# Two layers of local attention and a bilinear unit on one core: the down weights' loads move from SyncE's DMA queue to GpSimd's

## The chip, the cores and the metric

The kernel runs on one core of one Trainium2 chip. The core has five engines with instruction queues of their own: TensorE (PE, matrix products; its weight loads are shown as PEld), VectorE (DVE), ScalarE (ACT), GpSimd (POOL) and SyncE (SP). DMAs are issued by an engine's queue and carried out by 16 DMA engines. The metric is the device time of one execution in microseconds (us), the median of several runs.

## The reference

The model has four half-layers on 2048 tokens of width D = 576, in bfloat16: attention, gated unit, attention, gated unit, each with a layer norm ahead and a residual behind. The attention looks at 8 positions, 2 apart, with 32 heads of 18 elements:

```python
def _A_ref(x, wqkv, wo):
    qkv = (x @ wqkv).reshape(B, S, 3, H, Dh)          # H = 32, Dh = 18
    idx = pos[:, None] - arange(8)[None, :] * 2        # position and seven before it
    logits = einsum("bhsd,bhswd->bhsw", q, k[idx]) * Dh ** -0.5   # masked where idx < 0
    o = einsum("bhsw,bhswd->bhsd", softmax(logits), v[idx])
    return o.reshape(B, S, D) @ wo

def _B_ref(x, w_gate, w_up, w_down):                   # F = 4608
    return ((x @ w_gate) * (x @ w_up)) @ w_down

x = x + _A_ref(layernorm(x), wqkv, wo)
x = x + _B_ref(layernorm(x), w_gate, w_up, w_down)
x = x + _A_ref(layernorm(x), wqkv, wo)
x = x + _B_ref(layernorm(x), w_gate, w_up, w_down)
```

All four use the same weights A and B.

## The kernel before

The 2048 tokens are 16 tiles of 128. They are worked on in 18 *sequences*; a sequence is one attention and the gated unit after it for one or two tiles. The first four have one tile each, the other 14 have two (256 tokens). All intermediate results stay on the chip. The gate and up weights (wg, wu, wgu_t) are loaded once, in six parts; the down weights (5.3 MB) do not fit beside them and are loaded anew in every sequence, 18 loads of 288 KB each (`load_wd`, L682), 324 in all, into six buffers wd0 to wd5 taken in turn.

*Gated unit* (`glu`, L632). A unit of work has 512 columns of PSUM: gate matmuls (L655, into pg), up matmuls (L655, into pu), the tails of the 576 rows (L666), then ACT copies the gate half (g_sb, L677) and DVE multiplies (h, L678). Units come in threes. After some units come the down matmuls of the same units (L699 with 512 columns, L700 with 64), and DVE adds the residual (L709, L714). This is a phase. A one-tile sequence has three phases of three units, a two-tile sequence two phases of nine units. A one-tile phase needs six loads, as many as there are buffers. A two-tile phase has nine loads, all entered into the plan ahead of the phase's first down step; the last three of them go over buffers that the first three have just filled, and wait for nothing but those landings. The down steps of the first three units and of the last three then read the same buffers.

*Attention* (`attention`, L378). Projections on PE (L407); on DVE, products of q with shifted k (L503) and their sums (L507 to L512); score sums over a head's elements on PE (L518); softmax on DVE and ACT (L540 to L551, result s); then the weights are brought to all rows of a head: in the first five sequences by PE (L557), in the other thirteen through DRAM (a_dram, L567, and four DMAs back into ab, L570). DVE multiplies with v and adds (L587, L602), PE multiplies with wo (L614), DVE adds the residual (L620). The layer norm ahead of each half is DVE statistics (L343), ACT (L349, L358), and a transpose on PE (L369, first five sequences) or by DMA (L362).

*Order.* Nothing is issued as it is written. Every step is entered with `op`: its engine, a cost in ns, the buffers that it reads and writes, and a priority. `Plan.run` (L69) then goes through the ready steps, takes the one that can start first by these costs, and emits it. So each engine's order of instructions, PE's too, is fixed when the kernel is built, from the planned costs; on the chip each engine takes its instructions in that order and waits by semaphores. A DMA is planned as an issue on SP, then bytes at 250 GB/s after whatever DMA was planned before, then 2000 ns (L114 to L116):

```python
if o.nbytes:
    dma = max(dma, o.end) + o.nbytes / 250.0
    o.ready = dma + 2000
```

Before the change SP issues every DMA: inputs, weights, the trips of the attention weights through DRAM, DMA transposes, the down weights and the output. A load of wd waits in SP's queue until PE has read the buffer's old content, and until the DMA eight issues earlier has landed. POOL has only fills and masks at the start.

The diff touches `Plan.run` and `load_wd` in `glu`; the kernel's main loop calls `attention` and `glu` for each sequence and then `Plan.run`.

Of the kernel before, what the change touches and what calls it, by code (L numbers as in the profile page):

```python
# [20 lines left out]
class Plan:  # L21
# [11 lines left out]
    def op(self, eng, cost, fn, r=(), w=(), prio=1, after=None, hold=None, free=None, margin=0, nbytes=0, use=None,  # L33
           pair=None, need=None):
        o = Op()
        o.eng, o.cost, o.fn, o.prio, o.hold, o.free = eng, cost, fn, prio, hold, free
        o.margin, o.idx, o.succ, o.order, o.nbytes = margin, len(self.ops), [], set(), nbytes
        o.lat, o.use, o.pair, o.need = self.LAT[eng], use, pair, need
        d = set()
        for k in r:  # L40
            d.update(self.wr.get(k, ()))
        for k in w:
            d.update(self.wr.get(k, ()))
            d.update(self.rd.get(k, ()))
        for k in r:
            self.rd.setdefault(k, []).append(o)
        for k in w:
            self.wr[k] = [o]
            self.rd[k] = []
        d.discard(o)  # L50
        o.deps = d
        if after is not None and after not in d:
            o.order.add(after)
        for p in d | o.order:
            p.succ.append(o)
        o.n = len(d | o.order)
        self.ops.append(o)
        return o
# [9 lines left out]

    def run(self, slots):  # L69
        clock = {e: 0.0 for e in self.LAT}  # L70
        dma = 0.0
        free = {k: [(0.0, i) for i in range(v)] for k, v in slots.items()}
        cand = [o for o in self.ops if o.n == 0]
        done = 0
        while cand:
            best = None
            for o in cand:
                t = 0.0
                for p in o.deps:
                    e = p.ready if p.eng != o.eng else p.end  # L80
                    if e > t:
                        t = e
                t += o.margin
                if o.hold is not None:
                    f = free[o.hold]
                    if not f:
                        continue
                    t = max(t, min(f)[0])
                if o.pair is not None:
                    if len(free["unit"]) < len(o.pair):  # L90
                        continue
                    t = max(t, min(free["unit"])[0])
                if o.need is not None:
                    t = max(t, o.need["at"])
                t = max(t, clock[o.eng])
                key = (t, o.prio, o.idx)
                if best is None or key < best[0]:
                    best = (key, o)
            assert best is not None, "the plan is stuck"
            (t, _, _), o = best  # L100
            cand.remove(o)
            if o.hold is not None:
                got = min(free[o.hold])
                free[o.hold].remove(got)
                o.use["slot"] = got[1]
            if o.pair is not None:
                for u in o.pair:
                    got = min(free["unit"])
                    free["unit"].remove(got)
                    u["at"], u["slot"] = got  # L110
            o.end = t + o.cost
            clock[o.eng] = o.end
            o.ready = o.end + o.lat
            if o.nbytes:  # L114
                dma = max(dma, o.end) + o.nbytes / 250.0
                o.ready = dma + 2000  # L116
            if o.free is not None:
                u = o.use
                u["last"] = max(u.get("last", 0.0), o.ready)
                u["left"] = u.get("left", 1) - 1  # L120
                if u["left"] == 0:
                    free[o.free].append((u["last"], u["slot"]))
            o.fn()
            done += 1
            for s in o.succ:
                s.n -= 1
                if s.n == 0:
                    cand.append(s)
        assert done == len(self.ops)
# [3 lines left out]
def kernel(  # L133
# [12 lines left out]
    nc = tc.nc  # L146
    _, S, D = A_x.shape
    F = B_w_gate.shape[1]
    P = 128
# [17 lines left out]
    NXS, NWD, NH, NXB, NB = 4, 6, 9, 3, 3  # L167
# [6 lines left out]
    wd_v = B_w_down.rearrange("(g t p) d -> g p t d", p=P, t=2)  # L174
# [5 lines left out]
    def sb(name, shape, dt=BF16):  # L180
        return consts.tile(shape, dt, name=name)
# [30 lines left out]
    wd = [sb(f"wd{i}", [P, 2, D]) for i in range(NWD)]  # L212
# [12 lines left out]
    op = pl.op  # L225
# [23 lines left out]
    def dma(dst, src):  # L249
        return lambda: nc.sync.dma_start(dst, src)  # L250
# [376 lines left out]
    wd_no = {"n": 0}  # L627
# [4 lines left out]
    def glu(j, t0, nst, last):  # L632
        n = nst * P
# [48 lines left out]
        def load_wd(g):  # L682
            b = wd_no["n"] % NWD
            wd_no["n"] += 1
            op("SP", 550, dma(wd[b][:], wd_v[g]), w=[f"wd{b}"], nbytes=P * 2 * D * 2, prio=5.5 + (g // 3 if j == 0 else 0))
            return b

        nph = 2 if nst == 2 else 3
# [32 lines left out]
        for ph in range(nph):  # L721
            hsl, wsl = {}, {}
            mine = range(ph * upp, (ph + 1) * upp)
            for u in range(ph * upp, (ph + 1) * upp, NB):
                us = (u, u + 1, u + 2)
                for m in us:
                    wsl[m] = [load_wd(m * fpu // 2 + g) for g in range(fpu // 2)]
                    units[m] = {}
                full(u, wg, "wg", pg, True, False, pair=tuple(units[m] for m in us))
                full(u, wu, "wu", pu, True, False)  # L730
                full(u + 1, wg, "wg", pg, True, False, need=units[u + 1])
                tails(us)
                hsl[u] = evac(u)
                full(u + 1, wu, "wu", pu, False, True)
                hsl[u + 1] = evac(u + 1)
                full(u + 2, wg, "wg", pg, False, True)
                full(u + 2, wu, "wu", pu, False, True)
                hsl[u + 2] = evac(u + 2)
            use = {"left": nst}
            for m in mine:  # L740
                down(m, hsl[m], wsl[m], ph, use)
            settle(ph, use)
# [52 lines left out]
```

## Time and profile before

| | us |
|---|---|
| median of 3 runs | 1096.94 (1095.88 to 1098.84) |
| the profiled execution | 1094.6 |
| its span, first to last instruction | 1092.5 |
| PE busy | 1057.1 |
| DVE busy | 761.4 |
| ACT busy | 364.1 |
| POOL busy | 5.9 (26 instructions) |
| wd: 324 loads, median from issue to landing | 3.4 |

The profile is one execution as the hardware recorded it. A row of a group names the line, the engine, the operation and its tiles, the count, then busy time and mean duration, then the engine's idle time ahead of these instructions and what ended it. A row of the timeline has the start in us from the span's start, the duration, and in brackets the idle time of the engine ahead of it and its releaser. "SPq" is SP's queue. Windows give each engine's busy time in a stretch, and the clock that was granted to TensorE as a share of the full one.

### The profile page before, as it was taken

Reading aid. Unit: us, or ns where it says so; the run is one execution under the profiler, and the core shown is the slowest. Engines: PE = TensorE matmul, PEld = TensorE weight load, DVE = VectorE, ACT = ScalarE, POOL = GpSimd, SP = SyncE. Lnnn points to the kernel's source line nnn. Section 1 sums busy time; section 2 is a strip of 40 time slices with the busy share of each in tenths; the row PEclk is TensorE's granted clock in tenths of the full one; section 3 lists DMA queues with packets and bytes.
Section 4 is the critical chain, followed back from the end, with each engine's and each line's share of the span. In section 5 each row is a group of like instructions: output and inputs, shape, how many; then the busy total and the mean of one; then the engine's idle time right before and its main releaser. Section 6 shows DMA issues by size and latency. Waiting matters only on the chain.

```text
span 1092.5 us, 25296 instructions
## 1 busy us (share of the span) xinstructions
PE 1057.1 (97%) x10812; PEld 792.8 (73%) x10812; DVE 761.4 (70%) x1347; ACT 364.1 (33%) x768; POOL 5.9 (1%) x26
## 2 busy tenths in 40 slices
PE   5889999999999999999999899999999999999998
PEld 4668887777777777777767677777787777777775
DVE  6688889697979868798978563785757867322222
ACT  7435254432244443323342222314242232211111
POOL 2000000000000000000000000000000000000000
PEclk9899999999999999999999999999999999999999
DMA  8954563633333532535361434342333323333331
GB/s 261 336 155 119 172 200 98 183 110 97 95 99 102 147 84 74 135 112 155 99 168 24 122 99 122 92 121 56 117 106 122 107 72 121 105 96 109 116 110 55
DMA packets 146239, 133.17 MB, mean 122 GB/s; under 512 B 42000, under 2 KB 145488, under 8 KB 146128
## 3 DMA queue, kind: packets, MB, share of 16 engines
q1 hardware_dynamic: 146128, 131.57, 41.9%
q8 instruction: 84, 1.38, 0.5%
q14 instruction: 27, 0.22, 0.1%
HBM read 118.96 MB, written 4.73 MB: 113 GB/s over the span
## 4 chain that ended last, share of the span: by engine, by line
PE 88%; DVE 5%; DMA 4%; SPq 1%; issue 1%; ACT 1%; DVEq 0%; ACTq 0%
PE pu L655 21%; PE pg L655 21%; PE pg L699 12%; PE pu L699 10%; PE pg L666 6%; PE pg L407 6%; PE pu L407 4%; PE pa L614 3%; PE acct L700 3%; DMA a_dram<-s 2%; DMA ab<-a_dram 1%; SPq L570 1%; DMA wraw<-in_A_wqkv_dram 1%; DVE h L678 1%; DVE prod L503 1%
## 5 line engine op out<-in xcount | busy, mean ns | idle before, releaser
L677 ACT CAST g_sb<-pg 128x512 bf16<-128x512 f32 x288 | 158.9, 586 | 493.6 <-PE pu L666 359.7
L655 PE MATMUL pg<-xnT_B,wg 128*128 128x256 bf16 (+1 forms) x2592 | 301.1, 262 | 1.1 <-ACT xnT_B L372 1.1
L655 PE MATMUL pu<-xnT_B,wu 128*128 128x256 bf16 (+1 forms) x2592 | 301.9, 262 | 0.1
L678 DVE TENSOR_TENSOR h<-pu,g_sb 128x512 bf16<-128x512 f32 x288 | 193.3, 684 | 130.6 <-ACT g_sb L677 74.8
L655 PEld LDWEIGHTS <-wu 128*128 128x128 bf16 x2592 | 225.2, 98 | 40.1 <-issue 16.5
L655 PEld LDWEIGHTS <-wg 128*128 128x128 bf16 x2592 | 230.2, 98 | 28.9 <-issue 1.5
L699 PE MATMUL pg<-wd,h 128*128 128x512 bf16 x648 | 231.9, 382 | 0.0
L700 PE MATMUL acct<-wd,h 128*128 128x64 bf16 x1152 | 222.4, 193 | 0.0
L699 PEld LDWEIGHTS <-h 128*128 128x128 bf16 x1152 | 113.0, 98 | 130.5 <-issue 1.1
L699 PE MATMUL pu<-wd,h 128*128 128x512 bf16 x504 | 191.5, 380 | 0.9 <-DVE h L678 0.9
L587 DVE TENSOR_TENSOR prod<-vT,ab 128x1280 bf16<-128x1280 bf16 (+1 forms) x127 | 94.0, 741 | 47.1 <-DMA ab<-a_dram 46.0
L407 PEld LDWEIGHTS <-wqkv 128*128 128x128 bf16 (+1 forms) x1260 | 98.7, 99 | 25.6 <-issue 14.5
L700 PEld LDWEIGHTS <-h 128*128 128x128 bf16 x1152 | 113.1, 98 | 2.1 <-issue 1.1
L503 DVE TENSOR_TENSOR prod<-qT,kT 128x2560 bf16<-128x2560 bf16 (+1 forms) x72 | 95.7, 1332 | 22.4 <-ACT kT L449 21.9
L602 DVE TENSOR_TENSOR oT<-oT,prod 128x1280 bf16<-128x1280 bf16 (+1 forms) x119 | 90.8, 763 | 3.2
L666 PE MATMUL pu<-xnT_B,wgu_t 64*128 64x256 bf16 (+1 forms) x648 | 79.7, 259 | 4.2 <-DVE h L678 4.2
L407 PE MATMUL pg<-xnT_A,wqkv 128*128 128x256 bf16 (+3 forms) x650 | 79.7, 265 | 2.5 <-ACT xnT_A L372 1.6
L666 PE MATMUL pg<-xnT_B,wgu_t 64*128 64x256 bf16 (+1 forms) x648 | 79.8, 259 | 0.0
L407 PE MATMUL pu<-xnT_A,wqkv 128*128 128x256 bf16 (+3 forms) x610 | 77.2, 266 | 0.1
L709 DVE TENSOR_TENSOR xf<-pg,xf 128x512 f32<-128x512 f32 (+1 forms) x40 | 27.4, 684 | 66.3 <-PE pg L699 58.4
L666 PEld LDWEIGHTS <-wgu_t 64*128 64x128 bf16 x1296 | 50.3, 94 | 27.8 <-issue 22.6
L614 PE MATMUL pa<-wo_p,oT 128*128 128x288 bf16 x310 | 48.2, 286 | 2.5 <-DVE oT L602 1.8
(91 smaller groups left out, 614.0 us busy)
## 6 DMA issues: line engine op xcount, KB each, us to landing
wd<-in_B_w_down_dram SPq DMA_DIRECT2D x324, 288.0 KB, 3.4
ab<-a_dram SPq DMA_DIRECT2D x52, 128.0 KB, 2.7
wg<-in_B_w_gate_dram SPq DMA_DIRECT2D x6, 768.0 KB, 9.4
wu<-in_B_w_up_dram SPq DMA_DIRECT2D x6, 768.0 KB, 10.7
out_dram<-xf SPq DMA_DIRECT2D x8, 288.0 KB, 5.4
wraw<-in_A_wqkv_dram SPq DMA_DIRECT2D x4, 432.0 KB, 5.5
xb<-in_A_x_dram SPq DMA_DIRECT2D x6, 288.0 KB, 4.6
a_dram<-s SPq DMA_DIRECT2D x13, 128.0 KB, 2.2
```

The costliest lines, as they stand in the source:

```text
L407: nc.tensor.matmul(bank(p_, u)[0:m, e * n:(e + 1) * n], lhsT=wqkv[r_, k, c0:c0 + m], rhs=xnT_A[r_, k, 0:n], start=start, stop=stop, skip_g ...
L503: nc.vector.tensor_tensor(late["prod"][p_ % 2][:, :, :, 0:n], q2, k2, op=ALU.mult)
L587: nc.vector.tensor_tensor(js(dst), js(vT[:, :, o0:o0 + n]), abw, op=ALU.mult)
L602: op("DVE", 60 + 3 * n, lambda i_=i_: nc.vector.tensor_tensor(oT[:, :, 0:n], oT[:, :, 0:n], late["prod"][i_ % 2][:, 0, :, 0:n], op=ALU.add ...
L614: nc.tensor.matmul(b()[:, 0:HD], lhsT=oT[:, t, i * P:(i + 1) * P], rhs=wo_p[:, t, hh * HD:(hh + 1) * HD], start=(t == 0), stop=(t == KT - 1))
L655: nc.tensor.matmul(pt[:, e * n:(e + 1) * n], lhsT=w_[:, k, ft * P:(ft + 1) * P], rhs=xT[:, k, 0:n], start=(first and k == 0 and e == 0), s ...
L666: nc.tensor.matmul(ps[:, e * n:(e + 1) * n], lhsT=wgu_t[r_, ft * P:(ft + 1) * P], rhs=xT[r_, KF, 0:n], start=(first and e == 0), stop=not ...
L677: op("ACT", 590, lambda: nc.scalar.copy(g_sb[gs][:, 0:ul], pg[use["slot"]][:, 0:ul]), r=[f"wg_{j}_{u}"], w=[f"g{gs}"], prio=0)
L678: op("DVE", 690, lambda: nc.vector.tensor_tensor(hb[hs][:, 0:ul], pu[use["slot"]][:, 0:ul], g_sb[gs][:, 0:ul], op=ALU.mult), r=[f"wu_{j}_{ ...
L699: nc.tensor.matmul((pg, pu)[i][use["slot"]][:], lhsT=lhs, rhs=wt[:, e % 2, 0:512], start=first, stop=fin)
L700: nc.tensor.matmul(acct[:, i * TL:(i + 1) * TL], lhsT=lhs, rhs=wt[:, e % 2, 512:D], start=(first and i == 0), stop=fin, skip_group_check=True)
L709: op("DVE", 690, lambda i=i, dst=dst: nc.vector.tensor_tensor(dst[:, 0:512], (pg, pu)[i][use["slot"]][:], xs_f[:, i0 + i, 0:512], op=ALU.add),
```

## The change

All wd loads but the first six are issued by POOL (`nc.gpsimd.dma_start`) in place of SP (`nc.sync.dma_start`). They are entered with an issue of 1100 ns in place of 550. The plan keeps a separate end of transfers for each of the two queues, the one of POOL at 200 GB/s. Buffers, counts, dependencies, priorities and all other steps are the same; as costs and queues differ, `Plan.run` arrives at another order on every engine. SP keeps 132 instructions of 382, POOL has 348 where it had 31.

```diff
     def run(self, slots):
         clock = {e: 0.0 for e in self.LAT}
-        dma = 0.0
+        dma = {"SP": 0.0, "POOL": 0.0}
...
             if o.nbytes:
-                dma = max(dma, o.end) + o.nbytes / 250.0
-                o.ready = dma + 2000
+                dma[o.eng] = max(dma[o.eng], o.end) + o.nbytes / (250.0 if o.eng == "SP" else 200.0)
+                o.ready = dma[o.eng] + 2000
...
         def load_wd(g):
             b = wd_no["n"] % NWD
             wd_no["n"] += 1
-            op("SP", 550, dma(wd[b][:], wd_v[g]), w=[f"wd{b}"], nbytes=P * 2 * D * 2, prio=5.5 + (g // 3 if j == 0 else 0))
+            first = wd_no["n"] <= NWD
+            eng, q = ("SP", nc.sync) if first else ("POOL", nc.gpsimd)
+            op(eng, 550 if first else 1100, lambda: q.dma_start(wd[b][:], wd_v[g]), w=[f"wd{b}"], nbytes=P * 2 * D * 2,
+               prio=5.5 + (g // 3 if j == 0 else 0))
             return b
```

After the change the lines behind `load_wd` stand three lower (L699 becomes L702).

## The prediction

> **What bounds the kernel now.** I read the page first (busy time, slices, DMA issues), then the windows in which TensorE's busy share falls, then the waits of the queues and the timeline at those places. Page:
>
> ```profile
> PE 1057.1 (97%) x10812; PEld 792.8 (73%) x10812; DVE 761.4 (70%) x1347; ACT 364.1 (33%) x768; POOL 5.9 (1%) x26
> ...
> PE   5889999999999999999999899999999999999998
> ...
> DMA  8954563633333532535361434342333323333331
> ...
> wd<-in_B_w_down_dram SPq DMA_DIRECT2D x324, 288.0 KB, 3.4
> ```
>
> TensorE (PE) is busy for 97% of the span, so all that a change of queues can win is the remaining 35 us. The first slices hold most of it: start-up, which the change leaves alone. The down weights come as 324 loads of 288 KB. Next the windows (columns: PE, PEld, DVE, ACT, POOL busy, then granted clock, DMA share, GB/s):
>
> ```profile
> 64.00:74.00 10.00, 5.67 (x77) 3.94 (x78) 9.28 (x25) 4.75 (x14) 0.00 (x0) 0.99 0.22 60
> 74.00:84.00 10.00, 10.00 (x142) 8.09 (x141) 7.20 (x19) 5.46 (x14) 0.00 (x0) 0.84 0.49 150
> 190.00:200.00 10.00, 10.00 (x158) 8.23 (x156) 7.03 (x14) 5.18 (x11) 0.00 (x0) 1.00 0.62 197
> 610.00:622.00 12.00, 8.34 (x84) 6.70 (x82) 2.44 (x4) 2.24 (x4) 0.00 (x0) 1.00 0.52 159
> 622.00:626.00 4.00, 3.58 (x21) 2.57 (x21) 3.93 (x6) 0.58 (x1) 0.00 (x0) 0.66 0.00 0
> ```
>
> After 45 us PE idles in two places only, near 64 to 74 and near 618 to 622, and each is followed by a stretch at a lower granted clock (0.84, 0.66). Now SyncE's (SP's) waits between 55 and 76 us, and what stands around 620 us:
>
> ```profile
> SPq L250 <- DVE xf L620: 12.9, 1, 12.9
> ```
>
> ```profile
> 604.25 5.63 SPq L250 DMA_DIRECT2D wd<-in_B_w_down_dram  x5
> 609.97 0.42 SPq L250 DMA_DIRECT2D out_dram<-xf  x1
> 610.45 0.46 SPq L567 DMA_DIRECT2D a_dram<-s  x1
> 615.90 2.70 SPq L570 DMA_DIRECT2D ab<-a_dram  x4
> ```
>
> ```profile
> 605.86 0.69 DVE L551 TENSOR_TENSOR s<-Lt,zs 128x512 bf16<-128x512 f32 x1
> ```
>
> ```profile
> 620.94 0.83 DVE L587 TENSOR_TENSOR prod<-vT,ab 128x1280 bf16<-128x1280 bf16 x1 [6.82 <-DMA ab<-a_dram]
> 621.68 0.68 DVE L678 TENSOR_TENSOR h<-pu,g_sb 128x512 bf16<-128x512 f32 x1
> ```
>
> ```profile
> 622.41 0.27 PE L666 MATMUL pu<-xnT_B,wgu_t 64*128 64x256 bf16 x1 [4.08 <-DVE h L678]
> ```
>
> Both idle places lead back to SP's one queue. At 57.9 us SP stands 12.9 us at the load of the next x, which waits for DVE; all later wd loads stand behind it, so the order of issue gives PE nothing of the gated unit to do until 76 us. At 606.5 us the attention weights (s) are ready, but their trip through DRAM is issued at 610.45, behind five wd loads; a DVE product that waits for them holds the h multiply behind it, and PE waits 4.08 us.
>
> **The change part by part.** The sum is made against the profiled execution: 1094.6 us, of which the span is 1092.5 and 2.1 lie around it; it is 2.3 below the median of 1096.94, and what the sum gives is carried over to the median.
>
> *Idle near 64 to 74 us.* The wd loads no longer stand behind the x load. In the built order, 96 more gate and up matmuls (L655), 24 tails and 14 down matmuls stand ahead of the third sequence's score sums (L518). Sixteen L655 matmuls take 0.89 us in the chain here, tails 0.054 us each, a down pair 0.245: 5.3 + 1.3 + 1.7 = 8.3 us of work for 5.46 us of gaps (1.85 + 0.62 + 0.50 + 2.50). Filled: -5.5. The clock of 0.84 in the next 10 us cost 10 x 0.16 = 1.6; gone too. Sum -7.1.
>
> *What is late next.* The order gives most of this back. Ahead of the score sums at 200.8 us both orders have the same matmuls (1152 of L655), and these sums need DVE's s, which ended at 196.6, and two transposes of xn, whose second input ACT ended at 197.6. PE used the time until 200.1 for down steps. If DVE and ACT come no earlier, PE runs dry, and the sums start at about 198.5 (197.6, the transpose 0.2, the copy 0.7): net -2.3. If DVE is pulled along, -7.1 stays; it idles 12 of the 60 us from 100 to 160, so there is room. If it is pushed back by what the fuller order puts ahead of the third sums (8.3 - 5.5 = 2.8 us later), +0.5. I take -2.3, the row as it stands; ends -7.1 and +0.5.
>
> *The trip at 610 us.* SP has out and the trip alone in its queue. s was ready 3.9 us before the issue, and the landing of 5.39 us stands against 1.7 to 3.1 in eleven of the other twelve trips: 6 us of lateness for a stall of 4.08. The stall goes, and with it the clock of 0.66 over 4 us (1.4): -5.4. Other end: 0, if POOL's loads in flight slow the trip as much.
>
> *324 - 6 = 318 loads on POOL.* SP is freed of 318 x 0.41 us of issues, none on PE's path. POOL has 26 instructions and 5.9 us of work, all in the first 45 us; now each load's issue, and its wait for the buffer (PE's last reader) and for an earlier landing, stands in its queue, and nothing but the next load is behind it. No row shows an issue on POOL. From below it is SP's own median for this load, 0.41 us; from above the longest, 1.50; a gain is excluded, as every load must be issued. I take 1.2, the issue of a DMA transpose (1199/1214/2235 ns), the heaviest issue that the trace has as a rule. What it may cost follows from the tightest stretch, the sequences of one tile. Their down phases start at 112.12, 121.52, 131.93, 141.39 and 150.91: every 9.7 us, six loads each, six buffers. The first is issued 0.68 us into a phase (112.80) and the sixth is needed 2.8 us into the next: 9.7 + 2.8 - 0.7 = 11.8 us. Six issues at pace p and 2.2 us from the end of an issue to the landing (2.6 at best, less 0.4) fit if 6p + 2.2 <= 11.8, p <= 1.6. At 1.2 the last load is there 2.4 us early: cost 0. Sequences of two tiles have nine loads in 30 us (down phases at 257.3 and 286.9) and more room. The Trainium skill, page SBUF — State Buffer, section on two separate sides, speaks against the step: descriptors of a DMA issued from GpSimd are written by GpSimd's cores, which VectorE locks out during its two-port modes, and its example grows from 620 to 3100 ns. By the same page tensor_tensor has no such mode, and nearly all of DVE's work here is that, so by the rule the sum stays; no run yet shows it either way.
>
> *Two pipes planned as if each had the DMA engines alone.* Thirteen trips and the transposes now meet wd packets that used to be ordered with them. A load takes 0.88 us at the 336 GB/s of the busiest slice; two legs a trip, so up to 1.8 us a trip, of which PE sees only what exceeds the h multiplies queued ahead: ends 0 and 8, taken 1.5. *Order elsewhere:* 24 to 40 L655 matmuls more (0.11 us each) ahead of the sums of the seventh to ninth sequence (attention 2.6 to 4.4 us later), while PE has the units themselves to do: ends 0 and 3, taken 1.0.
>
> Sum: -2.3 - 5.4 + 0 + 1.5 + 1.0 = -5.2; profiled 1089.4, median 1096.94 - 5.2 = 1091.7, say 1092. By the ends -12.5 to +11.5 with p below 1.6.
>
> **The rivals.**
> *A, slower: POOL's pace.* If an issue on POOL takes more than 1.6 us, PE waits for wd in the one-tile sequences, 6p - 9.7 us for each of about 8 dense phases. PE then is not early at 190, so -7.1 counts whole: at p = 2, -7.1 + 18.4 - 5.4 + 2.5 = +8.4, 1105; at 2.2, +18, 1115. It turns the sign from p = 1.83 on. For it: 256 rows of 1152 bytes are more than any POOL instruction did before. Against: SP's 0.41 us for the same rows. Should DVE's two-input work lock POOL out (18.1 of 20 us busy from 120 to 140), half an L503 of 1.48 us on top of 1.2 gives 1.94, 8 x 1.94 = 15.5, -10 + 15.5 = +5.5, 1102: A with a smaller price.
> *B, no change: the gain is given back.* All 7.1 come back at 195 to 208 as waits for DVE, and the trip's stall moves to another trip: 0 - 2.7 + 2.5 = 0, 1097. For it: DVE is busy 33 of 40 us from 160 to 200. The skill's page DMA: Bandwidth & Descriptors, rules for kernel authors, would say this too: queues share 16 engines, spreading saves only issue time. The trace disagrees so far, as SP's 12.9 us are a wait in a queue and no issue.
> *C, slower without A: trips in traffic.* Three of thirteen stall as at 622 (5.4 each) with the gain at 70 given back: -2.3 + 11 = +8, 1105. For it: the one stall was such a one. Against: no other trip left PE idle for over 0.3 us.
>
> **How the numbers follow.** Forecast 0.46, A 0.24, B 0.21, C 0.09. About 0.3% (3.3 us) is what a measurement of this kernel tells from no change: faster is under 1093.6, slower over 1100.2. Faster 0.46, same 0.21, slower 0.33. Range: forecast down to -11 (1086), A and C up to p = 2.1 or +13 (1110); left out are 0.05 below and 0.13 above. The forecast's own range is 1087 to 1094.
>
> **What would show it.** Right: no PE idle between 64 and 76 us, a wait of PE for ACT's xn or DVE's s of 3 to 5 us near 192 to 200, no L666 wait near 622, POOL's issues under 1.6 us, SP's wait for L620 with no wd behind it. Wrong: PE waiting at L702 for DMA wd between 50 and 190 us (A); waits of L587 for ab longer than 6.8 us, with h and PE behind them (C); idle at 195 as large as that removed at 70 (B).

## The result and the profile after

The changed kernel takes 1101.67 us (median of 20 runs, 1094.97 to 1106.08) against 1095.24 for the kernel before on the same chip (20 runs, 1093.47 to 1100.51). The ratio is 1.0051 with an interval of 1.0037 to 1.0066: slower by half a per cent, where the forecast was 0.5% faster (5.2 of 1096.94 us). The profiled execution took 1100.58 us, 6.0 more than that of before; its span is 1098.6 against 1092.5.

From the page after (busy shares, slices, DMA queues with packets, MB and share of the engines' time, the costliest group of POOL, the issues with KB and median landing):

```profile
PE 1059.0 (96%) x10812; PEld 793.6 (72%) x10812; DVE 761.4 (69%) x1347; ACT 364.4 (33%) x768; POOL 235.1 (21%) x344
...
PE   5899999899999999999999999999999999999998
...
DMA  8963573533263514445252434331343333333330
...
q0 software_dynamic: 25440, 93.80, 27.7%
q1 hardware_dynamic: 59632, 37.77, 13.9%
...
L687 POOL DMA_DIRECT2D wd<-in_B_w_down_dram x318 | 229.3, 723 | 834.0 <-PE acct L703 768.2
...
wd<-in_B_w_down_dram POOLq DMA_DIRECT2D x318, 288.0 KB, 4.6
```

The 318 loads are on POOL's queue (q0) and cost 0.72 us of POOL each; POOL waits for PE, not PE for POOL. A load now lands after 4.6 us where it took 3.4. PE's busy time is 1.9 us longer, its idle time makes up the rest.

The windows of the changed kernel (PE, PEld, DVE, ACT, POOL busy, granted clock, DMA share, GB/s):

```profile
64.00:74.00 10.00, 9.78 (x169) 8.79 (x169) 9.25 (x25) 4.77 (x14) 1.74 (x3) 1.00 0.56 183
...
164.00:174.00 10.00, 7.15 (x44) 4.76 (x43) 7.07 (x10) 5.88 (x11) 0.00 (x0) 0.66 0.25 45
200.00:208.00 8.00, 4.82 (x46) 3.63 (x47) 5.78 (x12) 6.95 (x14) 3.38 (x5) 0.79 1.06 302
380.00:390.00 10.00, 8.07 (x81) 6.39 (x79) 9.86 (x14) 2.01 (x5) 0.00 (x0) 1.00 0.17 34
428.00:436.00 8.00, 5.48 (x56) 4.45 (x53) 7.90 (x13) 0.93 (x3) 0.00 (x0) 1.00 0.00 0
```

The last four of the same windows in the kernel before:

```profile
164.00:174.00 10.00, 10.00 (x119) 7.96 (x117) 8.62 (x14) 4.84 (x11) 0.00 (x0) 1.00 0.52 140
200.00:208.00 8.00, 7.47 (x86) 6.11 (x84) 6.86 (x14) 5.48 (x11) 0.00 (x0) 1.00 0.88 273
380.00:390.00 10.00, 10.00 (x95) 8.07 (x94) 9.08 (x19) 4.58 (x12) 0.00 (x0) 1.00 0.01 2
428.00:436.00 8.00, 8.00 (x72) 5.28 (x71) 7.65 (x12) 2.84 (x8) 0.00 (x0) 1.00 0.00 0
```

The idle place at 64 to 74 us is gone: PE is busy for 9.78 of 10 us there, where it was 5.67. But PE now stands still in the other four, where before it was busy for 10.00, 7.47, 10.00 and 8.00 us, and two of them bring a low clock (0.66, 0.79). All idle times of PE over 0.4 us after the first 45 us, read from PE's timeline, with what ended them:

| place, us (before / after) | before | after | ended after the change by |
|---|---|---|---|
| 64 to 74 | 5.47 | 0.81 | a load of wd, the only one that PE waited for |
| 167 | 0 | 2.85 | two DMA transposes, and ACT behind the first of them (below) |
| 201 to 204 | 0.53 | 4.14 | ACT's xn and xnT_B |
| 262 | 0 | 0.60 | DVE's h |
| 388 | 0 | 1.93 | DVE's h, behind a trip |
| 433 | 0 | 2.52 | DVE's h, behind a trip |
| 565 / 577 | 0.85 | 1.99 | a DMA transpose |
| 622 / 629 | 4.08 | 1.02 | DVE's h, behind a trip |
| 914 | 0.50 | 0 | DVE's h, behind a trip (before) |
| sum | 11.4 | 15.9 | |

These 4.4 us more of idle time and PE's 1.9 us more of busy time make 6.3 us, where the span is 6.1 longer; the shorter pauses and the start make up the difference.

How such a place comes about is seen at 433 us. The chain of the changed kernel there (start, duration, what):

```profile
416.48 0.61 DVE s L551
...
417.11 5.97 DMA a_dram<-s
...
424.40 2.68 DMA ab<-a_dram
...
427.20 0.82 DVE prod L587
...
432.73 0.69 DVE h L678
...
433.47 1.03 PE pu L655 x8
```

and the DVE timeline beside it (in brackets the idle time ahead and its releaser):

```profile
419.94 0.69 DVE L678 TENSOR_TENSOR h<-pu,g_sb 128x512 bf16<-128x512 f32 x1 [1.06 <-PE pu L655]
427.20 0.82 DVE L587 TENSOR_TENSOR prod<-vT,ab 128x1280 bf16<-128x1280 bf16 x1 [6.57 <-DMA ab<-a_dram]
...
432.73 1.28 DVE L678 TENSOR_TENSOR h<-pu,g_sb 128x512 bf16<-128x512 f32 x2
```

This store is not late in SP's queue: s ends at 417.08 and the store is issued at 417.11. But it takes 5.97 us instead of the 1.70 that it takes on a quiet stretch, and it does so beside six loads that POOL issued from 412.58 to 416.9. DVE stands 6.57 us at the product L587, the next h stands behind it in DVE's fixed order, and PE waits for that h. The thirteen stores of this one trace sort themselves by the loads in flight while the store itself is under way: with seven, six and five loads 7.42, 5.97 and 4.61 us; with none to two, 1.70 to 2.49. The slowest of them, at 366 us, was also issued 1.14 us after its s, behind two transposes.

At 167 us it is the transposes. They were issued at 157.19 and 158.76, between loads of POOL, and took 7.85 and 8.01 us. Two waits of PE end at nearly the same moment: the second transpose lands at 166.77, and ACT's g_sb, which the PE timeline names as releaser, ends at 166.81. ACT was late itself, as its next xn goes into the buffer that the first transpose was still reading; it stood 5.12 us. The transposes from issue to landing, and ACT's row:

```profile
L362 SPq DMA_TRANSPOSE xnT_A<-xn x2: 1276/1294/1311, 157.2 to 158.8; - x2
...
DMA to landing us min/median/max: 7.9/7.9/8.0
```

```profile
165.13 0.87 ACT L358 ACTIVATE xn<-xf,nmr,rstd 128x576 bf16<-128x576 f32 x1 [5.12 <-DMA xnT_A<-xn]
```

One more transpose, issued at 301.94, took 11.0 us, and no idle time of PE follows from it.

### The profile page after: what moved, and what is told of

The parts are those of the page before. It is cut to its first block, busy times and chain, and to the rows that moved or that the text cites. A ratio compares the mean times of both kernels' runs of the same rounds, so it can differ in the third digit from the quotient of the medians.

```text
span 1098.6 us, 25308 instructions
## 1 busy us (share of the span) xinstructions
PE 1059.0 (96%) x10812; PEld 793.6 (72%) x10812; DVE 761.4 (69%) x1347; ACT 364.4 (33%) x768; POOL 235.1 (21%) x344
## 4 chain that ended last, share of the span: by engine, by line
PE 85%; DMA 6%; DVE 5%; ACT 1%; issue 1%; SPq 1%; POOL 0%; DVEq 0%; ACTq 0%; POOLq 0%
PE pu L655 22%; PE pg L655 21%; PE pg L702 11%; PE pu L702 9%; PE pg L666 6%; PE pg L407 5%; PE pu L407 4%; PE pa L614 4%; PE acct L703 3%; DMA a_dram<-s 2%; DMA xnT_A<-xn 1%; DMA ab<-a_dram 1%; DVE prod L587 1%; DVE oT L602 1%; DMA wd<-in_B_w_down_dram 1%
## 5 line engine op out<-in xcount | busy, mean ns | idle before, releaser
L687 POOL DMA_DIRECT2D wd<-in_B_w_down_dram x318 | 229.3, 723 | 834.0 <-PE acct L703 768.2
L702 PE MATMUL pg<-wd,h 128*128 128x512 bf16 x648 | 230.1, 380 | 0.8 <-DMA wd<-in_B_w_down_dram 0.8
L702 PEld LDWEIGHTS <-h 128*128 128x128 bf16 x1152 | 112.7, 98 | 129.4
L702 PE MATMUL pu<-wd,h 128*128 128x512 bf16 x504 | 191.5, 380 | 0.6 <-DVE h L678 0.6
L587 DVE TENSOR_TENSOR prod<-vT,ab 128x1280 bf16<-128x1280 bf16 (+1 forms) x127 | 94.2, 742 | 49.0 <-DMA ab<-a_dram 48.0
```

The lines of the kernel that those rows point to most:

```text
L587: nc.vector.tensor_tensor(js(dst), js(vT[:, :, o0:o0 + n]), abw, op=ALU.mult)
L687: op(eng, 550 if first else 1100, lambda: q.dma_start(wd[b][:], wd_v[g]), w=[f"wd{b}"], nbytes=P * 2 * D * 2, prio=5.5 + (g // 3 if j == 0 ...
L702: nc.tensor.matmul((pg, pu)[i][use["slot"]][:], lhsT=lhs, rhs=wt[:, e % 2, 0:512], start=first, stop=fin)
```

## The experiments

The theory after the result: the transfers of SP's queue (trips and transposes) collide with POOL's loads, and the new order, planned as if each queue had the DMA engines to itself, has not enough work ahead of what waits for them. The rivals: POOL's queue itself is what costs (its issues, its collisions), whatever the order; or the new order is worse by itself, whatever the transfers.

### The queue without the order, and the order without the queue

```diff
 # e1: kernel before, its plan unchanged
-            op("SP", 550, dma(wd[b][:], wd_v[g]), ...)
+            q = nc.sync if wd_no["n"] <= NWD else nc.gpsimd
+            op("SP", 550, lambda: q.dma_start(wd[b][:], wd_v[g]), ...)
 # e2: kernel after, its plan unchanged
-            eng, q = ("SP", nc.sync) if first else ("POOL", nc.gpsimd)
+            eng, q = ("SP", nc.sync) if first else ("POOL", nc.sync)
```

> The queue alone: every engine's order is planned as before the change (one pipe, issue of 550 ns), but all wd loads except the first six are issued by POOL. Theory 1 (collision: DMA transposes and the trips through DRAM take 5 to 11 us where POOL's loads are in flight, 2.6 and 1.7 where not, and h multiplies wait behind them): transposes over 6 us appear, PE idles 2 to 5 us more than before after 80 us, ratio 1.002 to 1.007. Theory 2 (the new order alone is at fault, its margins are too thin for the chip): ratio 0.994 to 1.000, since SP's queue is free and the stall at 622 us goes while the order is the tried one.

> The order alone: planned as after the change, but SP issues all loads, in the planned sequence. Theory 1: no transpose stands beside a load that was issued after it, so none over 6 us; ratio 0.995 to 1.002, unless SP stands at a load's buffer with a trip behind it. Theory 2: the same stalls as after the change near 167, 388, 433 and 577 us; ratio 1.004 to 1.008.

The old order with POOL's queue: 1114.07 us, ratio 1.0147 (1.0123 to 1.0170). The new order with SP's queue alone: 1101.92 us, 1.0037 (1.0023 to 1.0051). Neither part is innocent: the queue alone cost twice what the collision had been expected to cost at most (1.007), and the order alone came out just under the range that had been given for it (1.004 to 1.008). In the old order the waits of DVE for ab, in total, times and longest, grow from 46.0, 12, 6.8 us to

```profile
DVE prod L587 <- DMA ab<-a_dram: 57.4, 12, 9.8
```

and PE has eight new idle places of 2.3 to 3.8 us after 200 us. In the new order with one queue the idle places are those of the changed kernel (1.1 us at 164, 4.1 near 197, 3.4 at 385, 2.6 at 431, 2.2 at 575, 1.4 at 629), although its transposes land within 5.4 us. One trip is late in SP's queue again (its store, at 365 us, was issued 3.84 us after s). The other two are not: the stores at 415 and 618 us were issued 0.59 and 0.17 us after s and took 5.36 and 4.85 us with five loads ahead of them in the same queue, much like the 5.97 and 4.61 us beside POOL's. With little traffic (the next runs) the same stores take 2.11 and 1.71 us. So they are late because the new order issues full loads just ahead of them, on either queue. So the new order is short of cover, that is of PE work placed ahead of what waits, whichever queue carries the loads: with the order given, POOL's queue adds 0.0014, within the intervals. Without a new order it costs 1.5%, so the replanning was worth about 1% against moving the loads alone.

### Both orders with little traffic

```diff
 # e3 (kernel after) and f1 (kernel before), all loads but the first six
-            q.dma_start(wd[b][:], wd_v[g])
+            q.dma_start(wd[b][:, :, 0:64], wd_v[g][:, :, 0:64])
```

> The changed kernel, its order and its queues, but POOL's loads bring only 64 of each row's 576 columns (32 KB in place of 288 KB, as many rows); the rest of each buffer keeps old weights, so part of the down product is left out. Theory 1: transposes 2.6 to 4 us, the stores of the trips under 3 us, ratio 0.990 to 0.997 (what the change would be worth without traffic). Theory 2: landings shorten, but PE still idles near 200, 388 and 433 us: ratio 1.003 to 1.006.

> The kernel before, order and queue, with all wd loads but the first six cut to 64 of 576 columns (part of the down product left out), issued by SP: what traffic costs before the change. If traffic costs both kernels alike, the ratio is 0.990 or less, as with the changed order (0.9889). If the old order meets little traffic, as the theory of the badly placed loads says, the ratio is 0.993 to 0.997: only the stall at 622 us (5.4 us with its clock) goes, and the gaps near 64 to 74 us stay.

The changed kernel with 64 of 576 columns loaded takes 1085.29 us, 0.9889 (0.9874 to 0.9904), a little under what the collision theory had expected (0.990 to 0.997); the kernel before, treated alike, 1085.40 us, 0.9903 (0.9883 to 0.9923). Instructions, orders and issues are those of the full kernels; only bytes are missing. Two things follow. First, without traffic the two orders are equal within the interval: the new one is 0.0014 lower, 1.5 us, give or take 3. In the new order the idle time near 192 to 196 us stays (4.1 us) and the places at 167, 388, 433 and 577 us are below 0.6 us or gone, so these are the traffic's and the first is not. Second, the traffic of wd costs 0.0097 of the time before (10.6 us) and 1.0051 - 0.9889 = 0.0162 after (17.8 us). The change made it 7 us dearer, give or take 3. With loads on SP the new order pays 1.0037 - 0.9889 = 0.0148 (16.2 us), with e3 standing for this order without traffic: most of the 7 us comes with the order.

f1 lies by the first case of its expectation (0.990 or less) and not by the second: the old order pays for its traffic too, and not only in the stall at 622 us. The span of f1 is 10.0 us shorter than that of the kernel before. PE's idle times over 0.4 us are 4.9 of these (6.5 in place of 11.4), and a mean granted clock of 0.995 in place of 0.991 is worth 4 more by estimate (0.004 of 1090).

### The collision by itself

A kernel of its own, with the shapes of the model but none of its computation: between gates that let the DMA engines go quiet it issues two transposes, or a store of s, or loads of wd, alone and side by side, each stretch five times.

```diff
+            gate(); tr()                            # two transposes alone (SP)
+            gate(); loads(nc.gpsimd); tr()          # beside three loads on POOL
+            gate(); loads(nc.scalar); tr()          # beside three loads on ACT's queue
+            gate(); tr(); loads(nc.sync)            # one queue, transposes first
+            gate(); loads(nc.sync); tr()            # one queue, loads first
+            gate(); loads(nc.gpsimd, 6); tr()       # beside six loads on POOL
+            gate(); trip()                          # the store alone; and so on
```

> A kernel that computes nothing of the model (its output is x): thirteen stretches, five times over, each opened by DVE with the DMA engines idle. Two DMA transposes alone: 2.6 us each. Beside three wd loads of POOL: theory 1 says 5 to 8 us, theory 2 says under 4. In one queue with the transposes first: 2.6 to 3 us for the transposes. Loads first in one queue: 4 to 5.5 us. Beside three loads on ACT's queue: 4 to 5 us if a second ring is enough, 2.6 to 3.5 if it takes POOL's kind of issue. The store of a trip: 1.7 us alone, 4 to 6 beside POOL's loads, under 2 ahead of loads in one queue. A load on POOL: 3.1 to 3.6 us alone, each further one 0.8 later.

From issue to landing, medians of the last four repeats, in us:

| stretch | first transpose | second | loads |
|---|---|---|---|
| alone | 2.58 | 2.59 | POOL 3.2 to 3.8, SP 2.9 to 3.6 |
| SP's queue, transposes first | 2.57 | 2.60 | 3.2 to 3.7 |
| SP's queue, loads first | 4.13 | 3.38 | 2.8 to 3.9 |
| three loads on POOL | 4.62 | 6.81 | 4.3 to 6.5 |
| three loads on ACT's queue | 5.30 | 5.15 | 3.2 to 5.1 |
| six loads on POOL | 4.29 | 7.43 | 4.0 to 7.2 |

The second queue takes away what the one queue gave for nothing. In a shared queue the transposes ahead of the loads keep their 2.6 us; with POOL they take up to 7.4, though in these stretches the first was issued about 0.1 us ahead of the loads. The queues of two stretches, the transposes alone (115 to 120 us) and beside POOL's three loads (134 to 142 us), with packets, MB and share of the engines' time:

```profile
q1 hardware_dynamic: 1344, 0.33, 32.6%
...
xnT<-xn SPq DMA_TRANSPOSE x2, 2.6
```

```profile
q0 software_dynamic: 239, 0.88, 41.4%
q1 hardware_dynamic: 1341, 0.33, 41.1%
...
wd<-in_B_w_down_dram POOLq DMA_DIRECT2D x3, 288.0 KB, 5.8
xnT<-xn SPq DMA_TRANSPOSE x2, 5.7
```

The same 0.33 MB of transposes holds the engines for 32.6% of 5 us, 1.6 us, alone, and for 41.1% of 8 us, 3.3 us, beside the loads. A packet of the transposes has 0.25 KB, one of POOL's loads 3.7 KB (0.88 MB in 239), one of the same loads from ACT's queue 1.1 KB (0.88 MB in 816). The Trainium skill, page DMA: Bandwidth & Descriptors, section Queues, rings and completion order, says that each DMA engine takes turns between the queues that have work, a whole packet at a time. The second transpose agrees with that: 6.8 us with POOL's larger packets, 5.1 with ACT's smaller ones. The first goes the other way (4.6 and 5.3), but ACT's first load was issued 0.1 us ahead of it and POOL's 0.1 us behind it. That the packet's size is the reason was not tried by itself.

The store alone took 1.71 us, behind three loads in SP's queue 3.9. The stretch with POOL's loads says little on it, as the store went out 0.1 us ahead of them (1.84).

### One clock for both queues in the plan

```diff
 # f2: kernel after
-                dma[o.eng] = max(dma[o.eng], o.end) + o.nbytes / (250.0 if o.eng == "SP" else 200.0)
-                o.ready = dma[o.eng] + 2000
+                dma["SP"] = max(dma["SP"], o.end) + o.nbytes / (250.0 if o.eng == "SP" else 200.0)
+                o.ready = dma["SP"] + 2000
```

> The changed kernel, loads on POOL, but the plan counts both queues' transfers on one clock, so that trips and transposes are planned behind the loads before them. If the change loses because the plan thinks each queue has the DMA engines alone, the stalls near 388, 433 and 577 us go and the ratio is 0.994 to 1.000. If not (a transpose is slowed by loads issued after it, which no clock in order of issue sees), the ratio stays at 1.003 to 1.010.

1085.18 us, ratio 0.9902 (0.9884 to 0.9920): faster than both kernels, with all bytes moved and the loads on POOL. After 80 us PE has no idle time over 0.4 us. The transfers are hardly better: transposes to 6.3 us, stores to 5.0, a trip's four legs to 8.0. What is better is what stands behind them. DVE's timeline of this kernel at the trip that answers to the one at 417 us:

```profile
399.53 0.69 DVE L551 TENSOR_TENSOR s<-Lt,zs 128x512 bf16<-128x512 f32 x1
409.42 0.69 DVE L712 TENSOR_TENSOR xf<-pg,xf 128x512 bf16<-128x512 f32 x1 [9.20 <-PE pg L702]
...
411.02 0.82 DVE L587 TENSOR_TENSOR prod<-vT,ab 128x1280 bf16<-128x1280 bf16 x1
```

This trip took 9.7 us beside six loads, as long as the 10.0 us of the changed kernel, and it cost nothing: in this plan, where the loads delay the trip, it lies beside down matmuls of PE (DVE waits 9.20 us for them, and the next h, at 413.31, waits for ACT and not for the products of L587), and PE works on. The idle time at 64 to 74 us is back as before (6.0 us), so the gain lies all behind it. The span is 14.0 us shorter than that of the changed kernel; 9.9 of these are idle times of PE over 0.4 us, and a granted clock of 0.994 in place of 0.990 is worth some 4 more by the same estimate.

### Lateness added by hand

```diff
 # f4: kernel after with 2000, f5: kernel before with 1000
+                if o.nbytes in (P_TRIP, P_TRANS):
+                    o.ready += 2000
```

> The changed kernel, loads on POOL, with one thing different in the plan: a transpose, a store of a trip and each of its loads back are planned to land 2 us later (4.6 us or more after their issue), so that h multiplies stand ahead of the products that wait. If the loss is PE waiting behind late transfers, PE's idle time after 210 us falls from 10 us to under 4 and the ratio is 0.992 to 0.999 although the transfers stay as slow as they are. If the loss is in the order's PE work or the clock, the ratio stays at 1.003 to 1.007.

> The kernel before, all loads on SP, with the same transfers planned to land 1 us later: whether such a margin alone is worth something without the second queue. Theory: the stall at 622 us goes (5.4 us), the 12.9 us wait of SP for x stays; ratio 0.993 to 1.000. Against: each attention comes later by the margin and PE runs dry elsewhere; 1.000 to 1.005.

Two clocks with 2 us more for each trip's and transpose's transfer: 1094.05 us, 0.9976 (0.9962 to 0.9990), 0.75% better than the changed kernel and inside the range expected. But the reason given for that range failed: PE's idle time after 210 us was to fall under 4 us, and it rose from 8.0 to 11.0, with 3.8 us at 378 and 2.7 at 935. The gain lies ahead of that, at 167 and 201 us (7.0 us became 1.7). The kernel before with 1 us more: 1094.61 us, 0.9981 (0.9968 to 0.9994); its place at 622 is gone and three others have come (2.4 us at 578, 3.0 at 595, 1.6 at 873). A fixed allowance helps a little and moves the stalls about.

### Is it the clock, or the deal?

`Plan.run` takes the step that can start first, so any other number deals another order. These four runs ask whether the shared clock won by what it says or by luck. h1: one clock, POOL's issue at the measured 720 ns. h2: one clock, all transfers at 150 GB/s. h3: two clocks, POOL at 250 GB/s and 720 ns. h4: two clocks, 150 GB/s each.

```diff
 # h1: from f2                          # h3: from the kernel after
-            550 if first else 1100      -  250.0 if o.eng == "SP" else 200.0;  550 if first else 1100
+            550 if first else 720       +  250.0;                              550 if first else 720
 # h2: from f2                          # h4: from the kernel after
-  250.0 if o.eng == "SP" else 200.0     -  250.0 if o.eng == "SP" else 200.0
+  150.0                                 +  150.0
```

> Changed kernel with one clock for both queues in the plan, and POOL's issue entered with the measured 720 ns in place of 1100: another order than the shared-clock run, by the same assumption on the DMA engines. Theory (two separate clocks make the plan optimistic and that costs the time): ratio below 0.995, no stall of h above 1 us near 388 or 433. Rival (the plan takes the first step that fits, so any small change of its numbers deals another order; the run at 0.990 was a good draw): anywhere from 0.99 to 1.01, with stalls at other places.

> One clock for both queues and 150 GB/s for all transfers in place of 250 and 200, issue 1100 ns: a still more cautious plan. Theory: below 0.995, since a plan that expects its transfers late puts more work ahead of what waits for them. Rival (a draw): 0.99 to 1.01, stalls at other places.

> Changed kernel with its two clocks, but POOL's transfers at 250 GB/s and its issue at 720 ns: more optimistic still. Theory: 1.003 to 1.015, stalls of h behind trips as in the changed kernel. Rival (a draw): 0.99 to 1.01, and it may well be below 0.995.

> Changed kernel with its two clocks, but each at 150 GB/s, so that the two together are about what the DMA engines carried in the busiest slices. Theory in its form 'the sum of the two pipes is too wide': below 0.998; in its form 'transfers must be ordered on one clock': above 1.000. Rival (a draw): 0.99 to 1.01.

All kernels in which the full loads are on POOL, each ratio against the kernel before on the same chip, with PE's idle times over 0.4 us in two parts and DVE's waits for ab at L587 (us):

| run | plan's clocks | ratio (interval) | PE idle 45 to 140 us | after 140 us | waits for ab |
|---|---|---|---|---|---|
| e1, old order | (SP alone) | 1.0147 (1.0123 to 1.0170) | 5.5 | 24.2 | 60.9 |
| the change | two | 1.0051 (1.0037 to 1.0066) | 0.8 | 15.0 | 53.2 |
| h3 | two, 250 GB/s | 1.0133 (1.0108 to 1.0158) | 0.9 | 24.0 | 62.2 |
| h4 | two, 150 GB/s | 1.0327 (1.0304 to 1.0350) | 24.8 | 11.9 | 54.6 |
| f4 | two, and 2 us | 0.9976 (0.9962 to 0.9990) | 0 | 12.7 | 38.6 |
| f2 | one | 0.9902 (0.9884 to 0.9920) | 6.0 | 0 | 26.7 |
| h1 | one, 720 ns | 0.9947 (0.9927 to 0.9966) | 6.0 | 0.8 | 26.5 |
| h2 | one, 150 GB/s | 1.0411 (1.0391 to 1.0430) | 34.6 | 13.7 | 25.6 |

The rows behind the last column for f2, h1, h3 and h2, in that order:

```profile
DVE prod L587 <- DMA ab<-a_dram: 26.4, 9, 4.9
...
DVE oT L587 <- DMA ab<-a_dram: 0.3, 1, 0.3
```

```profile
DVE prod L587 <- DMA ab<-a_dram: 26.5, 9, 4.6
```

```profile
DVE prod L587 <- DMA ab<-a_dram: 57.1, 12, 8.5
...
DVE oT L587 <- DMA ab<-a_dram: 5.1, 1, 5.1
```

```profile
DVE prod L587 <- DMA ab<-a_dram: 25.6, 6, 9.6
```

The trace of h1 is that of its fastest execution (1084.62 us, median 1088.85, slowest 1095.79), so its idle times are those of a good case.

At 200 to 250 GB/s the expectation came out: one clock 0.990 and 0.995, two clocks 1.005 and 1.013, and the more optimistic plan of each pair is the slower. In the waits for ab the split holds in all three pairs, 26 us with one clock and 53 to 62 with two. In the time it does not: h2 was expected below 0.995 and is 4% slower, and h4, though above 1.000 as one form of the theory has it, is so for the same other reason. Their loss is in the start. From 46 to 140 us (PE, PEld, DVE, ACT, POOL busy), in h2 and then in the kernel before:

```profile
46.00:140.00 94.00, 59.89 (x622) 45.22 (x622) 59.04 (x138) 31.77 (x76) 10.52 (x15) 0.75 0.27 80
```

```profile
46.00:140.00 94.00, 88.54 (x1335) 72.41 (x1333) 74.61 (x164) 36.22 (x85) 0.00 (x0) 0.98 0.57 173
```

PE does 29 us less work in that time, and waits for DVE's attention steps with no matmuls of the gated unit put beside them. That a plan which expects the gate and up weights late holds the units back is likely, but was only argued. Of h2's 13.7 us after 140, 11.7 are one place: a transpose issued at 218.56 us among five loads of POOL took 12.03 us. A single collision can outlast the cover that even this plan left.

So the rival has its share. A single order's time can't be told from the plan's numbers, two draws a side at 200 to 250 GB/s are few, at 150 GB/s the plan with one clock is the slower of the two (1.0411 and 1.0327), and the kernel before, with one clock and one queue, has 46.0 us of these waits itself. What the runs bear out is narrower: with the loads on POOL, the waits for ab were twice as long with two clocks as with one in each of the three pairs.

## Why the prediction was wrong

**The step that failed** is "Two pipes planned as if each had the DMA engines alone", taken at +1.5 us between ends of 0 and 8. It counted the bytes of a load, 0.88 us for each leg of a trip, and asked what exceeds the h multiplies ahead. Measured are stores of 7.4 and 6.0 us where 1.70 is the quiet time, and transposes of 7.9 and 8.0 where 2.6 is: 4 to 6 us of lateness at once, not 1.8, and in an order with less ahead of them. The step looked for the cost in packets that meet; the new order on one queue shows nearly the same loss (1.0037), so what it had wrong is the cover that an order planned in this way leaves ahead of such waits. By the runs with little traffic, the wd traffic costs 7 us more than before (10.6 to 17.8, give or take 3). The forecast's terms for it, the trip at 610 us (-5.4) and this one (+1.5), made -3.9. The 11 us between are about the whole distance from the forecast's -5.2 us to the measured +5.6 us (0.0051 of 1095). The transposes were named in the step and not priced, and two of the places (167, 577 us; 4.8 us idle) are theirs. The trace of before had the sign: PE idle for 0.85 us at 565 us behind a transpose, one of the places that "two places only" passed over.

**Idle near 64 to 74 us, and what is late next: right.** 5.47 us became 0.81 (-4.7; -5.5 was forecast), and PE ran dry at 201 to 204 us for 4.14 us, waiting for ACT's xn and its copy, the wait of 3 to 5 us that the forecast named, somewhat later than its 192 to 200, as the place at 167 lies ahead of it (without traffic it stands at 192 to 196). Net of the two -1.1 us in idle time, and the order by itself is worth 1.5 us without traffic, give or take 3, where -2.3 was taken. The low clock moved along with the idle time (0.84 at 74 to 84 before, 0.79 at 200 to 208 after), so the 1.6 us for it were not won.

**The trip at 610 us: right in kind, too large.** The store is issued 0.03 us after s, but takes 4.61 us beside five loads; PE's 4.08 us became 1.02 at 629. That is -3.1 of the -5.4; what the other end had named ("if POOL's loads in flight slow the trip as much") happened at the trips near 366 and 417 us.

**318 loads on POOL at 0: right.** The issue takes 0.72 us (722/722/838 ns from shortest to longest), not the 1.2 that was taken, and far from 1.6. PE's one wait for a load in the whole span:

```profile
PE pg L702 <- DMA wd<-in_B_w_down_dram: 0.8, 1, 0.8
```

Rival A is out. The Trainium skill's page SBUF — State Buffer, section on two separate sides, lets VectorE lock out GpSimd's descriptor writing only in modes that tensor_tensor doesn't have; with DVE busy for 69% of the span, some 85% of it with tensor_tensor, the issues of 722 to 838 ns agree with that.

**Rival B** named the return at 195 to 208, which came. The rule named with it (the Trainium skill, DMA: Bandwidth & Descriptors, rules for kernel authors: spreading loads over queues saves only issue time) was kinder than the chip: e1, where the queue alone changes, lost 1.5%. **Rival C** ("trips in traffic", given 0.09) had the mechanism that decided it. C asked for three trips that stall as at 622; there are three new or remaining stalls of h behind trips (388, 433, 629 us), 1.9, 2.5 and 1.0 us and so smaller than its 5.4, with the transposes added. The test that the forecast set for it, a wait of L587 above 6.8 us, is not met (6.8 is the longest again): the same wait simply had less work of PE ahead of it. The reason held against C, "no other trip left PE idle for over 0.3 us", was not quite so (0.50 us at 914, for an h behind the trip of 904) and was read in the old order. A trip of 10.5 us near 403 us stood in that trace too, with DVE waiting 6.7 us for it, and PE had work enough. That row said how near the edge the trips were, and the change dealt the order anew.

## What to carry to other kernels

Moving transfers to a second queue frees the first queue's order, but also gives up its protection: transposes issued ahead of the bulk loads are no longer served ahead of them. Where a planner fixes the order, try one clock in its model for all queues that share the DMA engines: two separate clocks cost 1.5% here between two kernels whose sources differ in nothing else, and 1.9% lie between h1 and h3. That is no rule, as at 150 GB/s it went the other way. Before trusting that a transfer is hidden, look at the waits that the trace shows on engines off the critical path (DVE's 6.8 us at L587): a new order decides whether they reach PE.

## What the runs showed of the hardware

- Two DMA transposes take 2.6 us alone or ahead of loads in their own queue, 4.6 and 6.8 beside three loads of 288 KB on POOL's queue, 5.3 and 5.1 beside three on ACT's, and single ones up to 11.0 in the changed kernel's traffic and 16.1 in that of h2.
- The same load is cut into packets of 3.7 KB when POOL issues it and of 1.1 KB from ACT's queue or SP's (0.88 MB in 816 packets for three loads on either). Alone it lands nearly as fast from POOL as from SP (3.2 to 3.8 and 2.9 to 3.6 us).
- POOL's issue of 256 rows of 1152 bytes takes 0.72 us, SP's 0.41. With rows of 128 bytes POOL's median was 720 ns: between these two the bytes of a row made no difference.
